# A six-layer cross network on one core: stores of two blocks, eighteen row loads, four more ScalarE parts

## The chip, the cores and the metric

The kernel runs on one core of one Trainium2 chip. Five engines take part: TensorE (PE, and PEld for its weight loads), VectorE (DVE), ScalarE (ACT), GpSimd (POOL) and SyncE (SP), which does no arithmetic and issues transfers. Transfers issued by SP or ACT are carried by the same sixteen DMA engines. The metric is the device time of one execution in microseconds; the median of three runs is compared.

## The reference

The input x0 has 4096 rows of 416 features (26 fields of 16), there are six square weight matrices of 416 x 416 and six bias rows, all in bf16. What is computed is the cross network

```
x = x0
for l in range(6):
    x = x0 * (x @ ws[l] + bs[l]) + x
```

Since every layer multiplies by the same x0, the sum can be kept in a factor c with x = x0 * c: c starts at one, and each layer adds x @ ws[l] + bs[l] to it. The kernel works with this factor.

## The kernel before, in words

**Layout.** In layers 0 to 4 the activations lie transposed: features on the 128 partitions, batch rows along the free axis. The 416 features are three full tiles of 128 (`XM0`, `XH`, `CM`) and a remainder of 32. Four batch groups of 512 rows share the partitions for the remainder (`XR`, `CR`), so its work is done on tiles of 128 partitions. The batch is in two halves `s` of 2048 rows. `CM` and `CR` hold the factor c, `XM0` and `XR[0]` hold x0, and two of the three `XH` buffers hold the present activations.

**Layers 0 to 4.** For each half and each feature tile, TensorE makes the products into PSUM, ScalarE evicts them with the bias as bf16 (L187), and VectorE adds to c (L188) and multiplies by x0 (L189). `rem_pair` does the same for the remainder, through `ew_rem`: there ScalarE evicts a tile of 512 columns in parts of 256 (L196), and VectorE adds (L202) and multiplies (L203) the whole tile. In layers 1 to 3 this comes after the first two feature tiles of the layer. Layer 4 (`feeding_layer`) has its own order, with VectorE's instructions pinned, and also sends c, with the last bias added, through DMA transposes into `XLrows`, where batch rows lie on the partitions.

**The last layer.** Now activations are the stationary operand, so results come out with 128 batch rows on the partitions: a block is 128 rows by 416 features, 104 KB in bf16, and there are 32 of them. They are made in four rounds of eight blocks (u = 0 to 7), each round in four PSUM tiles of two blocks. In rounds one and two (`PAIRS`) two blocks of one tile are evicted together. In round three (`TURNS`) a group is two blocks of two tiles, evicted one by one. In round four (`ENDS`) each block goes through alone, so that the last one has little behind it. The steps of a group are in `ew` and `close_product`: ScalarE copies PSUM to bf16 (L507); VectorE adds c from `XLrows` (L511); when the next group has come to the same point, VectorE multiplies by x0 from `X0rows` into a tile `o` (L494); and the store to the output is issued (L496). For u = 5 to 7 of round four TensorE adds c itself, so that L511 is left out, and for u = 7 VectorE reads PSUM directly (`direct`) and ScalarE issues the store. All other stores are issued by SP.

**Stores.** A store's size is set by `parts`, the blocks per transfer:

```
            for j in range(0, n, parts):
                eng.dma_start(out_v[:, rows(q, g0 + j, parts), :], o[:, j:j + parts, :])
```

`parts` is `n // len(srcs)`. A group evicted at one go is stored in one transfer of two blocks (208 KB): nine of these. The three groups of round three that were evicted in two goes are stored block by block, as are the eight of round four: 14 transfers of 104 KB, 13 by SP and one by ScalarE.

**Order.** Every engine runs its instructions in its own order and waits on semaphores. SP's order is: the transposing loads of x0, weights, `X0rows` in twelve loads (L133), four rows of the last bias (L135), then nothing until layer 4, then eight DMA transposes (L231, L379), then the stores. Transfers take eight completion semaphores in turn; a transfer waits until the one eight before it has landed. The kernel ends (L573) when SP has seen the landing of every transfer and the engines have met.

Of the kernel before, what the change touches and what calls it, by code (L numbers as in the profile page):

```python
# [9 lines left out]
ACT = mybir.ActivationFunctionType  # L10
ALU = mybir.AluOpType
BF16 = mybir.dt.bfloat16
# [4 lines left out]
def kernel(  # L17
# [7 lines left out]
    nc = tc.nc  # L25
    B, D = x0.shape
    L = ws.shape[0]
    P = 128
# [5 lines left out]
    CW = 512  # L34
    SW = NG * CW
    NBT = B // P
# [5 lines left out]
    opool = ctx.enter_context(tc.tile_pool(name="opool", bufs=10))  # L42
# [3 lines left out]
    out_v = out.rearrange("(bt p) d -> p bt d", p=P)  # L46
# [10 lines left out]
    bR = const.tile([P, L], FP32)  # L57
    X0rows = big.tile([P, NBT, D], BF16)
# [14 lines left out]
    def load_wm(eng, l):  # L73
        eng.dma_start(WM[:, l], ws[l, 0:NK * P, :].rearrange("(k p) n -> p k n", p=P))
# [5 lines left out]
    def pin(ins):  # L80
        tc.keep_in_program_order(ins)
# [33 lines left out]
    for g in range(1, NG):  # L115
        dst, src = WR[32 * g:32 * g + 32, 0, :], WR[0:R, 0, :]
# [11 lines left out]
        load_wr(nc.sync, g, 1, L)  # L128
    for l in range(2, L):
        load_wm(nc.sync, l)  # L130
    for q in range(12):
        b0, b1 = NBT * q // 12, NBT * (q + 1) // 12
        nc.sync.dma_start(X0rows[:, b0:b1, :], x0_v[:, b0:b1, :])  # L133
    for g in range(NG):
        nc.sync.dma_start(bLr[32 * g:32 * g + 1, :], bs[LL:LL + 1, :])  # L135
# [55 lines left out]
    def ew_rem(l, s, pr, nxtR):  # L191
        cols = slice(CW * s, CW * s + CW)
        halves = [slice(a, a + CW // 2) for a in range(0, CW, CW // 2)]
        base = CR[:, cols] if l == 0 else tpool.tile([P, 2 * CW], BF16, name="t")
        for a in halves:
            nc.scalar.activation(base[:, a], pr[:, a], ACT.Identity, bias=bR[:, l:l + 1], scale=1.0)  # L196
        if l == 0:
            for a in halves:
                part = slice(CW * s + a.start, CW * s + a.stop)
                pin(nc.vector.tensor_tensor(out=nxtR[:, part], in0=CR[:, part], in1=XR[0][:, part], op=ALU.mult))  # L200
            return
        nc.vector.tensor_tensor(out=CR[:, cols], in0=base[:, 0:CW], in1=CR[:, cols], op=ALU.add)  # L202
        nc.vector.tensor_tensor(out=nxtR[:, cols], in0=CR[:, cols], in1=XR[0][:, cols], op=ALU.mult)  # L203
# [30 lines left out]
    def first_layer(s):  # L234
# [53 lines left out]
        for m in range(2):  # L288
            ew_main(0, s, m, 1, pb[m], nxt)
        ew_rem(0, 0, pr[:, 0, :], nxtR)  # L290
        ew_main(0, s, 2, 1, pb[2], nxt)
        ew_rem(0, 1, pr[:, 1, :], nxtR)

    bias_setup()
# [4 lines left out]
    def rem_pair(l, cur, curR, nxtR):  # L299
        pr2 = psum.tile([P, 2, CW], FP32, tag="ps", name="pr2")  # L300
        for s in range(NS):
            mm_rem(l, s, pr2[:, s, :], cur, curR)
        for s in range(NS):
            ew_rem(l, s, pr2[:, s, :], nxtR)
# [140 lines left out]
    l = LL  # L445
# [8 lines left out]
    def mm_q_open(q, g, py):  # L454
        for k in range(NK):
            for j in range(0, P, 32):
                nc.tensor.matmul(py[j:j + 32, 0:D], lhsT=q_x(q, g, k)[:, j:j + 32], rhs=WM[:, l, k, :],  # L457
                                 start=(k == 0), stop=False, tile_position=(0, j))

    def mm_q_full(q, g, py, closes, adds=False):  # L460
        s, i = quads[q]
        for k in range(NK):
            nc.tensor.matmul(py[:, 0:D], lhsT=q_x(q, g, k), rhs=WM[:, l, k, :],  # L463
                             start=((not closes) and k == 0), stop=(closes and not adds and k == NK - 1))
            if adds:
                c0 = col0(s, g) + 128 * i
                nc.tensor.matmul(py[:, P * k:P * k + P], lhsT=CM[:, k, c0:c0 + 128], rhs=ident[:], start=False, stop=False)
        if adds:
            nc.tensor.matmul(py[:, NK * P:D], lhsT=CR[:, CW * s + 128 * i:CW * s + 128 * i + 128],
                             rhs=ident[:, 32 * g:32 * g + 32], start=False, stop=True)  # L470

    def mm_q_rem(q, py, done):
        s, i = quads[q]
        biased = s == NS - 1 and i >= 2
        for g in range(NG):
            nc.tensor.matmul(py[g][:, 0:D], lhsT=curR[32 * g:32 * g + 32, CW * s + 128 * i:CW * s + 128 * i + 128],  # L476
                             rhs=WR[32 * g:32 * g + 32, l, :], start=(g >= done), stop=(not biased and g < done),
                             tile_position=(32 * g, 0))
        for g in range(NG if biased else 0):
            nc.tensor.matmul(py[g][:, 0:D], lhsT=ones[32 * g:32 * g + 1, :],  # L480
                             rhs=bLr[32 * g:32 * g + 1, :], start=False, stop=(g < done), tile_position=(32 * g, 0))

    pending = []

    def rows(q, g0, n):
        s, i = quads[q]
        b0 = 16 * s + 4 * g0 + i
        return slice(b0, b0 + 4 * (n - 1) + 1, 4)

    def close_product():  # L490
        while pending:
            src, q, g0, n, parts, eng = pending.pop()
            o = opool.tile([P, 2, D], BF16, name="o")
            pin(nc.vector.tensor_tensor(out=o[:, 0:n, :], in0=src, in1=X0rows[:, rows(q, g0, n), :], op=ALU.mult))  # L494
            for j in range(0, n, parts):
                eng.dma_start(out_v[:, rows(q, g0 + j, parts), :], o[:, j:j + parts, :])  # L496

    def ew(q, g0, srcs, eng, added, direct):
        if direct:
            close_product()  # L500
            pending.append((srcs[0], q, g0, 1, 1, eng))
            return
        t = tpool.tile([P, 2 * CW], BF16, name="t")
        n = 0
        for src in srcs:
            w = src.shape[1]
            nc.scalar.copy(t[:, n * D:n * D + w * D].rearrange("p (a d) -> p a d", a=w), src)  # L507
            n += w
        tv = t[:, 0:n * D].rearrange("p (a d) -> p a d", a=n)
        if not added:  # L510
            pin(nc.vector.tensor_tensor(out=tv, in0=tv, in1=XLrows[:, rows(q, g0, n), :], op=ALU.add))  # L511
        close_product()
        pending.append((tv, q, g0, n, n // len(srcs), eng))

    PAIRS = [(0, 0), (0, 1), (1, 0), (1, 1), (2, 0), (2, 1), (3, 0), (3, 1)]
    TURNS = [(0, 0), (0, 1), (1, 0), (2, 0), (3, 0), (1, 1), (2, 1), (3, 1)]
# [2 lines left out]
    for q, at, done in rounds:  # L519
        tiles = [psum.tile([P, 2, CW], FP32, tag="ps", name=f"py{n}") for n in range(4)]  # L520
        bank = [tiles[n][:, a, :] for n, a in at]

        final = q + 2 == NQ

        def close(groups):
            u, direct = groups[0][0], final and groups[0][0] == 7
            srcs = [tiles[at[g[0]][0]][:, at[g[0]][1]:at[g[0]][1] + len(g), 0:D] for g in groups]
            ew(q + u // 4, u % 4, srcs, nc.scalar if direct else nc.sync,
               final and u >= 5, direct)

        for u in range(done):
            if q == 0:
                mm_q_open(q, u, bank[u])
            else:
                mm_q_full(q, u, bank[u], False)
        mm_q_rem(q, bank[0:4], done)
        close([range(done)])
        if q == 0:
            last_rows_out()
        mm_q_rem(q + 1, bank[4:8], 0)  # L540
        for u in range(done, 8):
            mm_q_full(q + u // 4, u % 4, bank[u], True, final and u >= 5)
            if at is ENDS:
                close([[u]])
            elif u % 2:
                close([[u - 1, u]] if at is PAIRS else [[u - 1], [u]])
    close_product()


# [28 lines left out]
```

## Time and profile before

| | |
|---|---|
| median of three runs | 129.44 us (129.32 to 129.5) |
| the profiled execution, its own time | 129.42 us |
| its span, first to last instruction | 127.5 us |
| busy in the span: PE, DVE, ACT | 122.6, 102.4, 87.7 us |
| stores issued by SP, first and last issue | 22, at 111.59 and 124.74 us |
| store issued by ScalarE (u = 7) | at 124.35 us |
| the `X0rows` loads, first issue and length on SP's queue | 23.07 us, 9.20 us |
| largest wait on SP's queue: for layer 4 | 58.1 us |

All positions are microseconds from the start of the span. The execution's own time is 1.9 us above the span. A share of busy time is an average over stages; what matters here is which wait ends last in a stage.

### The profile page before, as it was taken

Reading aid. Unit: us, or ns where it says so; the run is one execution under the profiler, and the core shown is the slowest. Engines: PE = TensorE matmul, PEld = TensorE weight load, DVE = VectorE, ACT = ScalarE, POOL = GpSimd, SP = SyncE. Lnnn points to the kernel's source line nnn. Section 1 sums busy time; section 2 is a strip of 40 time slices with the busy share of each in tenths; the row PEclk is TensorE's granted clock in tenths of the full one; section 3 lists DMA queues with packets and bytes.
Section 4 is the critical chain, followed back from the end, with each engine's and each line's share of the span. In section 5 each row is a group of like instructions: output and inputs, shape, how many; then the busy total and the mean of one; then the engine's idle time right before and its main releaser. Section 6 shows DMA issues by size and latency. Waiting matters only on the chain.

```text
span 127.5 us, 3953 instructions
## 1 busy us (share of the span) xinstructions
PE 122.6 (96%) x1684; PEld 55.3 (43%) x1686; DVE 102.4 (80%) x192; ACT 87.7 (69%) x109; POOL 5.1 (4%) x18
## 2 busy tenths in 40 slices
PE   7999999999999999999999999999999999999970
PEld 3343343444544354434443544354434445445440
DVE  0124579774979898989898989898999999999990
ACT  0138866887858577859577859576859697679650
POOL 4004001400000000000000000000000000000000
PEclk9999999999999999999999999999999999999999
DMA  3999999999950000000000000000097999899864
GB/s 84 256 228 218 184 241 258 295 332 333 338 169 0 5 0 0 8 0 5 0 5 0 5 0 0 5 0 5 0 86 168 173 152 215 177 274 300 264 197 153
DMA packets 42229, 16.37 MB, mean 128 GB/s; under 512 B 31034, under 2 KB 42212, under 8 KB 42212
## 3 DMA queue, kind: packets, MB, share of 16 engines
q1 hardware_dynamic: 37432, 15.40, 53.5%
q10 hardware_dynamic: 4780, 0.72, 3.6%
q8 instruction: 13, 0.21, 0.7%
q14 instruction: 4, 0.03, 0.1%
HBM read 6.15 MB, written 3.41 MB: 75 GB/s over the span
## 4 chain that ended last, share of the span: by engine, by line
PE 90%; DMA 4%; ACTq 2%; DVEq 1%; issue 0%; ACT 0%; DVE 0%
PE pt L208 50%; PE py L463 12%; PE ph L240 11%; PE pt L214 5%; PE pr L224 5%; DMA xrig<-in_x_dram 4%; PE pr L220 2%; PE py L476 2%; PE ph L247 2%; PE py L457 1%; ACTq L86 1%; DVEq L573 1%; ACTq L108 1%; ACT t L507 0%; PE tpr L163 0%
## 5 line engine op out<-in xcount | busy, mean ns | idle before, releaser
L208 PE MATMUL pt<-XH,WM 128*32 128x512 bf16 x1152 | 65.2, 379 | 0.0
L187 ACT ACTIVATE t<-pt,bM 128x1024 bf16<-128x1024 f32 x36 | 37.2, 1116 | 13.7 <-PE pt L214 13.7
L208 PEld LDWEIGHTS <-WM 128*32 128x32 bf16 x1152 | 29.7, 97 | 33.8 <-issue 5.1
L188 DVE TENSOR_TENSOR CM<-t,CM 128x1024 bf16<-128x1024 bf16 x36 | 24.7, 686 | 4.3 <-ACT t L187 4.3
L189 DVE TENSOR_TENSOR XH<-CM,XM 128x1024 bf16<-128x1024 bf16 x36 | 24.9, 692 | 2.6
L507 ACT CAST t<-py 128x416 bf16<-128x416 f32 (+1 forms) x22 | 14.2, 649 | 4.2 <-PE py L463 2.0
L463 PE MATMUL py<-WM,XH 128*128 128x416 bf16 x90 | 17.0, 339 | 0.0
L240 PE MATMUL ph<-XM,WM 128*128 128x512 bf16 x70 | 16.3, 379 | 0.1
L332 ACT ACTIVATE t<-pt,bM 128x1024 bf16<-128x1024 f32 x12 | 12.4, 1115 | 4.1 <-PE pt L214 4.1
L181 ACT ACTIVATE CM<-ph,bM 128x1024 bf16<-128x1024 f32 x12 | 12.5, 1114 | 3.5 <-PE ph L247 3.5
L183 DVE TENSOR_TENSOR XH<-CM,XM 128x512 bf16<-128x512 bf16 x24 | 8.8, 428 | 4.2 <-ACT CM L181 4.2
L463 PEld LDWEIGHTS <-XH 128*128 128x128 bf16 x90 | 8.5, 98 | 7.5 <-issue 1.2
L240 PEld LDWEIGHTS <-WM 128*128 128x128 bf16 x72 | 6.8, 98 | 8.5 <-issue 1.1
L494 DVE TENSOR_TENSOR o<-t,X0rows 128x832 bf16<-128x832 bf16 (+1 forms) x19 | 9.4, 504 | 0.1
L511 DVE TENSOR_TENSOR t<-t,XLrows 128x832 bf16<-128x832 bf16 (+1 forms) x17 | 8.9, 521 | 0.0
L340 DVE TENSOR_TENSOR CM<-t,CM 128x1024 bf16<-128x1024 bf16 x12 | 8.0, 685 | 0.3 <-ACT t L332 0.3
L344 DVE TENSOR_TENSOR XH<-CM,XM 128x2048 bf16<-128x2048 bf16 (+1 forms) x7 | 7.5, 1067 | 0.2
L214 PE MATMUL pt<-XR,WR 32*128 32x512 bf16 x96 | 7.3, 379 | 0.0
L224 PE MATMUL pr<-XH,WM 128*32 128x512 bf16 x96 | 6.6, 379 | 0.0
L196 ACT ACTIVATE t<-pr,bR 128x256 bf16<-128x256 f32 x12 | 4.7, 475 | 1.6 <-PE pr L224 1.6
L114 ACT ACT_TABLE_LOAD x1 | 1.3, 1283 | 6.0 <-DMA XM<-in_x_dram 6.0
L224 PEld LDWEIGHTS <-WM 128*32 128x32 bf16 x120 | 3.2, 97 | 3.2
(61 smaller groups left out, 58.7 us busy)
## 6 DMA issues: line engine op xcount, KB each, us to landing
X0rows<-in_x_dram SPq DMA_DIRECT2D x8, 312.0 KB, 7.3
out_dram<-o SPq DMA_DIRECT2D x9, 208.0 KB, 3.0
WM<-in_ws_dram SPq DMA_DIRECT2D x5, 312.0 KB
out_dram<-o SPq DMA_DIRECT2D x13, 104.0 KB, 2.2
X0rows<-in_x_dram SPq DMA_DIRECT2D x4, 208.0 KB, 6.0
WR<-in_ws_dram SPq DMA_DIRECT2D x4, 130.0 KB, 5.1
WM<-in_ws_dram ACTq DMA_DIRECT2D x1, 312.0 KB
XM<-in_x_dram SPq DMA_TRANSPOSE x8, 5.6
```

What stands on the lines that cost most here:

```text
L181: nc.scalar.activation(c, src, ACT.Identity, bias=bias, scale=1.0)
L187: nc.scalar.activation(t[:], src, ACT.Identity, bias=bias, scale=1.0)
L188: nc.vector.tensor_tensor(out=c, in0=t[:], in1=c, op=ALU.add)
L189: nc.vector.tensor_tensor(out=x, in0=c, in1=XM0[:, m, c0:c0 + 2 * CW], op=ALU.mult)
L208: nc.tensor.matmul(pts[g // 2][32 * q:32 * q + 32, g % 2, :], lhsT=WM[:, l, k, 128 * m + 32 * q:128 * m + 32 * q + 32], rhs=cur[s][:, k, C ...
L214: nc.tensor.matmul(pts[g // 2][:, g % 2, :], lhsT=WR[32 * g:32 * g + 32, l, 128 * m:128 * m + 128], rhs=curR[32 * g:32 * g + 32, CW * s:CW ...
L224: nc.tensor.matmul(pr[32 * g:32 * g + 32, :], lhsT=WM[:, l, k, NK * P:D], rhs=cur[s][:, k, CW * g:CW * g + CW], start=False, stop=(k == NK ...
L240: nc.tensor.matmul(pt[:, gl, :], lhsT=WM[:, 0, k, 128 * m:128 * m + 128], rhs=cur[:, k, c0:c0 + CW], start=(k == 0 and not after_row), sto ...
L332: nc.scalar.activation(ts[t + (h,)][:], pts[t][h][:].rearrange("p a b -> p (a b)"), ACT.Identity, bias=bM[:, t[1], l:l + 1], scale=1.0)
L463: nc.tensor.matmul(py[:, 0:D], lhsT=q_x(q, g, k), rhs=WM[:, l, k, :], start=((not closes) and k == 0), stop=(closes and not adds and k == ...
L494: pin(nc.vector.tensor_tensor(out=o[:, 0:n, :], in0=src, in1=X0rows[:, rows(q, g0, n), :], op=ALU.mult))
L507: nc.scalar.copy(t[:, n * D:n * D + w * D].rearrange("p (a d) -> p a d", a=w), src)
```

## The change

Three edits, which meet only in SP's queue.

The output tile `o` is now taken when a group is closed, not when its product is made, and a store covers the whole tile. So a group of two blocks in round three goes in one transfer. In round four, blocks 0 and 1, 2 and 3, 4 and 5 share a tile each: each product goes into its own half, and the store is issued after the second one. Blocks 6 and 7 are stored alone as before, 7 by ScalarE. SP's stores become 16: fifteen of two blocks and one of one.

`X0rows` is loaded in eighteen transfers (four of one block, fourteen of two) where there were twelve (four of two blocks, eight of three).

In `ew_rem`, the second half's tile (s = 1) in layers 1 and 2 is evicted in four parts of 128 columns where there were two of 256: four more ScalarE instructions in all.

```diff
-    for q in range(12):
-        b0, b1 = NBT * q // 12, NBT * (q + 1) // 12
+    for q in range(18):
+        b0, b1 = NBT * q // 18, NBT * (q + 1) // 18
         nc.sync.dma_start(X0rows[:, b0:b1, :], x0_v[:, b0:b1, :])
...
-        for a in halves:
-            nc.scalar.activation(base[:, a], pr[:, a], ACT.Identity, bias=bR[:, l:l + 1], scale=1.0)
+        n = CW // (4 if s and l in (1, 2) else 2)
+        for a in range(0, CW, n):
+            nc.scalar.activation(base[:, a:a + n], pr[:, a:a + n], ACT.Identity, bias=bR[:, l:l + 1], scale=1.0)
...
-    pending = []
+    pending, outs = [], []
...
     def close_product():
         while pending:
-            src, q, g0, n, parts, eng = pending.pop()
-            o = opool.tile([P, 2, D], BF16, name="o")
-            pin(nc.vector.tensor_tensor(out=o[:, 0:n, :], in0=src, in1=X0rows[:, rows(q, g0, n), :], op=ALU.mult))
-            for j in range(0, n, parts):
-                eng.dma_start(out_v[:, rows(q, g0 + j, parts), :], o[:, j:j + parts, :])
-
-    def ew(q, g0, srcs, eng, added, direct):
+            src, q, g0, n, o, j, last, eng = pending.pop()
+            pin(nc.vector.tensor_tensor(out=o[:, j:j + n, :], in0=src, in1=X0rows[:, rows(q, g0, n), :], op=ALU.mult))
+            if last:
+                eng.dma_start(out_v[:, rows(q, g0 - j, j + n), :], o[:, 0:j + n, :])
+
+    def ew(q, g0, srcs, o, j, last, eng, added, direct):
         if direct:
             close_product()
-            pending.append((srcs[0], q, g0, 1, 1, eng))
+            pending.append((srcs[0], q, g0, 1, o, j, last, eng))
             return
...
-        pending.append((tv, q, g0, n, n // len(srcs), eng))
+        pending.append((tv, q, g0, n, o, j, last, eng))
...
         def close(groups):
-            u, direct = groups[0][0], final and groups[0][0] == 7
+            u = groups[0][0]
             srcs = [tiles[at[g[0]][0]][:, at[g[0]][1]:at[g[0]][1] + len(g), 0:D] for g in groups]
-            ew(q + u // 4, u % 4, srcs, nc.scalar if direct else nc.sync,
-               final and u >= 5, direct)
+            paired = final and u < 6
+            j = u % 2 if paired else 0
+            if not j:
+                outs.append(opool.tile([P, 2, D], BF16, name="o"))
+            ew(q + u // 4, u % 4, srcs, outs[-1], j, bool(j) or not paired, nc.scalar if final and u == 7 else nc.sync,
+               final and u >= 5, final and u == 7)
```

## The prediction

> **What bounds the kernel now.** I read the page's busy times and slices first, then the chain that ended last, then SP's queue and the DMA engines over the last 4 us.
>
> ```profile
> PE 122.6 (96%) x1684; PEld 55.3 (43%) x1686; DVE 102.4 (80%) x192; ACT 87.7 (69%) x109; POOL 5.1 (4%) x18
> ...
> PE   7999999999999999999999999999999999999970
> ...
> 122.91 0.52 ACT t L507
> 123.42 0.02 issue
> 123.44 0.06 DVE o L494
> ```
>
> TensorE is busy without a gap up to 123.6 us; no edit touches its instructions. So only two things can move the time: a new gap in TensorE's row, or the 4 us tail behind it. In the tail the chain leaves TensorE at block u=6's eviction (122.91), goes to its product (123.44), and on to u=7's product and store. SP's queue and the landings stand behind that:
>
> ```profile
> 123.76 0.40 SPq L496 DMA_DIRECT2D out_dram<-o  x1
> ...
> 124.35 0.38 ACTq L496 DMA_DIRECT2D out_dram<-o  x1
> ...
> 124.74 0.39 SPq L496 DMA_DIRECT2D out_dram<-o  x1
> ...
> SPq L573 <- DMA out_dram<-o: 1.3, 3, 0.6
> ```
>
> The store at 124.74 is u=6's, yet its product ended at 123.44 + 0.38 = 123.82. SP was late: it issued u=0 to u=6 at 121.86, 122.30, 122.77, 123.26, 123.76, 124.25, 124.74, one per 0.44 to 0.49 us, each after the one before and not after its product. By the semaphore events, u=7's store (124.35) has landed at 126.31, u=6's at 126.63; SP's last waits follow at 126.64 and 126.70, and the span ends at 127.50, 0.87 us after the last landing. The end is therefore the issue backlog of SP.
>
> One thing limits what an earlier issue can bring. The sixteen DMA engines are not level:
>
> ```profile
> DMA  0006994269963799628993199952999999999600
> GB/s 17 25 25 216 415 308 125 75 216 308 291 167 92 233 291 283 200 92 275 333 325 92 50 283 275 275 158 92 308 374 316 333 366 341 283 275 300 208 25 0
> ```
>
> These are the DMA engines from 122.4 to 126.4 us in slices of 0.1 us: bursts of some 0.35 us, one per store, with valleys between, until the last three run together from 125.1. In the valley at 122.4 one engine alone still moves (17 to 25 GB/s). It fell behind at 116.34, when an instruction fetch of 16 KB took one engine for 0.95 us: of the sixteen parts of the ninth store (issued 117.79) fifteen have landed by 120.04, the last at 121.39. From there that part comes at 121.70, 122.03, 122.36, 122.67, 123.04, 123.44, 124.13 (u=0; another fetch of 0.31 us began at 122.81), 124.50 (u=1), 124.81, 125.15, 125.53 (u=4). Only at u=4 has it caught up with the other fifteen (125.51).
>
> **The change part by part.**
>
> Round three: 10, 11 and 12 lose one SP issue each (0.33 to 0.45 us). They are issued as soon as their product is ready, and that stays (118.51, 119.57, 120.44); the second halves leave up to 0.42 us earlier. Nothing waits for them.
>
> Round four, SP's queue: seven issues become four. A two-block issue costs 0.42 to 0.46 us in the rows at 112.65 to 114.26, a one-block issue 0.33 to 0.41. The products end at u=1 121.66, u=3 122.80, u=5 123.37, u=6 123.82, and a store starts 0.03 us after its product when SP is free. So: u0+1 at 121.69, u2+3 at 122.83, u4+5 at 123.40, free at 123.85, u6 at 123.90 instead of 124.74, a move of 0.84 us. Only u=2's data leaves later, by 0.06 us. There is a 0.44 us hole in SP's queue ahead of u=0's store (121.42 to 121.86, product long done) that the trace doesn't name. If it falls on u4+5 instead, u6 goes at 124.34, still ahead of u=7's store. A slower issue under full DMA queues (0.97 and 1.23 us at 111.59 and 116.47) bounds it from above: +0.8 us on u4+5 puts u6 back at 124.7, no gain; I take 0.45, since the last seven issues all cost 0.33 to 0.41.
>
> The end by the last landing: u=7's store depends on its product (124.31) and stays at 124.35. On fifteen engines it landed by 126.28 with u=5's burst beside it, so 126.1 to 126.3 now; 1.74 us, the shortest flight in the tail, would be 126.09. On the lagging engine everything after u=1 (124.50) is now queued early: six blocks at 0.315 us each (steps of 0.31 to 0.33 while it was never idle; a pair saves one completion write of 0.009) end at 124.50 + 1.89 = 126.39. Bounds: 0.33 a block gives 126.48, no lag 126.28. I take 126.39, as that engine shows these very steps. u=7's semaphore is waited for last, so the wait at 126.64 falls away: 126.39 + 0.81 = 127.20, against 127.50: −0.30 us.
>
> The Trainium skill's "DMA: Bandwidth & Descriptors", section "Anatomy of one DMA — SWDGE (gpsimd) path", gives a transfer a fixed 2.0 us plus bytes over 436 GB/s, mostly the receipt of the last write: an estimate of 2.24 us for one block. By it u=7 would land at 126.59 and the change bring 0.04 to 0.10 us. Here one-block stores issued by SP from 122.77 on took 1.74 to 2.04 us, so the rule, given for another issuing path, is too long for them.
>
> Row loads: six more issues on SP. Twelve took 9.20 us from 23.07, one each 0.47 to 1.22 us; in that stretch the engines are full (some 330 GB/s), so the bytes, unchanged, set the pace. Six more cost between 0 and 6 x 0.9 = 5.4 us of SP's queue; I take 1. Behind them on SP stand the bias rows (needed at 118.5) and the first transpose at 92.84, before which SP waits 58.1 us; the rows are first used at 108.8. That cover makes the cost nothing; without it, up to 5.4 us. POOL issues no transfer.
>
> The completion semaphores are taken in turn, and six more loads and six fewer stores leave u=7 on the one it had. ScalarE's wait on it was met at 123.44, 0.9 us ahead of need; now it is that of store nine, 121.39. With 17 instead of 20 output tiles over ten buffers, reuse waits get shorter too.
>
> ScalarE parts: no 128-column eviction is in the trace. Of the neighbours, 256 columns start every 0.36 us, 1024 every 1.0, which extrapolates to 0.25. Four of 0.25 for two of 0.36 is +0.28 us per layer; bounds 0 and +0.72 (each as long as 256). It ends ahead of these idle times:
>
> ```profile
> 36.95 2.12 ACT L187 ACTIVATE t<-pt,bM 128x1024 bf16<-128x1024 f32 x2 [1.33 <-PE pt L214]
> ...
> 36.64 0.42 DVE L202 TENSOR_TENSOR CR<-t,CR 128x512 bf16<-128x512 bf16 x1
> ...
> 56.18 1.11 ACT L187 ACTIVATE t<-pt,bM 128x1024 bf16<-128x1024 f32 x1 [1.33 <-PE pt L214]
> ```
>
> ScalarE then waits 1.33 us for TensorE, and the add that consumes the parts starts at 36.64, 1.0 us after the last part ended (35.62). Cost nothing; if the cover failed, TensorE would wait for a PSUM buffer by what exceeds it.
>
> Sum: 129.42 − 0.30 = **129.12 us**, 0.32 below the median of 129.44 (which is 0.02 above the profiled execution), or 0.25%. About 0.2%, 0.26 us, is what can be told from no change.
>
> **The rivals.**
>
> A (the forecast): the backlog goes, the lagging engine sets the end. With the bounds above, 126.28 + 0.81 to 126.48 + 0.87: 129.01 to 129.27 us.
>
> B: the lagging engine isn't behind any more when u=7 comes. For it: it had caught up at u=4 before. Against: it had idle time only by the backlog that now goes. Then u=7's own flight is all: 126.09 + 0.81, −0.6 at most: 128.82 to 129.01.
>
> C: nothing is won, because u=7's store flies longer among the pairs. For it: u=0 and u=1 took 2.27 and 2.20 us. At 2.2 us it lands at 126.55, −0.14 by the same working; u4+5's issue stretched by 0.8 us brings u6 back to where it was, 0. A few hundredths either way: 129.2 to 129.6. The 2.24 us of the Trainium skill's "DMA: Bandwidth & Descriptors", above, would be this case.
>
> D, the other side: the pair u4+5 is still in flight when u6 and u7 come. For it: two-block stores took 2.6, 2.8 and 3.2 us, the ninth 3.6. On its slowest engine u6 and u7 follow it 0.32 us apart. With u4+5 (issued 123.40) in flight for 2.6 us they end at 126.64, level with before; from 2.9 us (126.94, +0.25 us) the kernel is slower, and 3.3 us gives 127.34, +0.65. Against: those stores flew among transposes and a fetch, at 300 GB/s. 129.7 to 130.1.
>
> E, that the change isn't made as said, is excluded by the code: `last` is true for every group but the first of a pair.
>
> **How the numbers follow.** A 0.50, of which 0.42 lies below 129.18 and 0.08 above; B 0.13; C 0.18; D 0.19. Faster by over 0.2%: 0.42 + 0.13 = 0.55. Within: 0.08 + 0.18 = 0.26. Slower: 0.19. The time is A's. The range runs from 128.88, inside B, to 129.60, the top of C, and leaves out D and B's low end. The faster cases alone span 128.82 to 129.18.
>
> **What would show it.** Right: 16 stores on SP, u6's issued near 123.9; the last landing u=7's, at 126.3 to 126.5, its sixteenth part trailing; no gap in TensorE's row; the loads of `X0rows` over long before 92. Wrong: an SP issue beyond 0.6 us after 122.8; a last landing after 126.6; TensorE waiting for PSUM near 37 or 56 us; TensorE's end away from 123.6, which would mean that the order of instructions has changed elsewhere.

## The result

| | before | after |
|---|---|---|
| median of seven runs | 129.50 us (129.32 to 129.66) | 129.01 us (128.89 to 129.24) |
| ratio, with its 95% interval | | 0.9964 [0.9952, 0.9976] |
| profiled execution, its own time | 129.42 us | 129.12 us |
| its span; time outside the span | 127.52; 1.90 us | 127.34; 1.78 us |
| start of u=7's product on VectorE | 123.73 us | 123.98 us |
| from there to the span's end, here called the tail | 3.79 us | 3.36 us |

The change makes the kernel faster, by 0.36%. The median lies 0.11 us under the predicted 129.12 us and inside the range. That the profiled execution also took 129.12 us is chance: the table shows that it started its end 0.24 us later than the profile of before, and gained 0.43 us in the tail and 0.12 us outside the span. The forecast of 0.30 us was for the tail alone.

The busy times of the page of after, its stores and its row loads, and then ScalarE's new parts from the groups by form (busy time, mean ns, idle time before them):

```profile
PE 122.9 (97%) x1684; PEld 55.3 (43%) x1686; DVE 102.4 (80%) x192; ACT 88.3 (69%) x113; POOL 5.1 (4%) x18
...
out_dram<-o SPq DMA_DIRECT2D x15, 208.0 KB, 2.9
...
L197 ACT ACTIVATE t<-pr,bR 128x128 bf16<-128x128 f32 x8 | 2.3, 381 | 0.0
```

TensorE has the same 1684 products; the order of instructions on every engine is that of before apart from the edits. ScalarE has four more instructions and 0.6 us more work, beside TensorE.

SP's stores at the end of after, one row each from the timeline (start us, length us), and ScalarE's store of u=7:

```profile
120.71 0.37 SPq L496 DMA_DIRECT2D out_dram<-o  x1
121.93 0.37 SPq L496 DMA_DIRECT2D out_dram<-o  x1
123.07 0.37 SPq L496 DMA_DIRECT2D out_dram<-o  x1
123.64 0.37 SPq L496 DMA_DIRECT2D out_dram<-o  x1
124.11 0.43 SPq L496 DMA_DIRECT2D out_dram<-o  x1
124.59 0.38 ACTq L496 DMA_DIRECT2D out_dram<-o  x1
```

These are group 12 of round three, u=0 and 1, 2 and 3, 4 and 5, 6, and 7. SP now starts each after its product, and u=6's store leaves ahead of u=7's. The landings confirm that u=7's comes last, at 126.51 us; u=6's came at 126.18.

The DMA engines of after from 122.6 to 126.6 us, in slices of 0.1 us (share in tenths, then GB/s):

```profile
DMA  0049999951000189999999999899999989700000
GB/s 17 25 166 366 358 349 349 358 175 25 0 0 0 58 291 308 308 283 308 341 308 308 308 300 341 300 308 317 333 358 325 283 275 291 215 8 0 0 0 0
```

What matters are the three empty slices from 123.6 to 123.9 us. There all sixteen engines have run dry, the late one too. From then on they are full until 126.0 us and end together: no slices with one engine alone (17 to 25 GB/s) follow, but for one of 8 GB/s.

The last waits of SP on landings, from 123 us on: in all, number of times, longest.

```profile
SPq L577 <- DMA out_dram<-o: 1.8, 4, 0.6
```

SP ends them at 126.59 us, 0.08 us after the last landing; in before it was 126.77, 0.14 us after.

Below, positions from different profiles are compared by shifting each so that u=7's product starts at 123.73 us, as in before; such a position is called relative.

### The profile page after: what moved, and what is told of

Its sections match the earlier page's. It is cut to its first block, busy times and chain, and to the rows that moved or that the text cites. A ratio compares the mean times of both kernels' runs of the same rounds, so it can differ in the third digit from the quotient of the medians.

```text
span 127.3 us, 3951 instructions
## 1 busy us (share of the span) xinstructions
PE 122.9 (97%) x1684; PEld 55.3 (43%) x1686; DVE 102.4 (80%) x192; ACT 88.3 (69%) x113; POOL 5.1 (4%) x18
## 4 chain that ended last, share of the span: by engine, by line
PE 90%; DMA 5%; SPq 1%; DVEq 1%; ACT 0%; issue 0%; DVE 0%
PE pt L209 50%; PE py L464 12%; PE ph L241 11%; DMA XM<-in_x_dram 5%; PE pt L215 5%; PE pr L225 5%; PE pr L221 2%; PE py L477 2%; PE ph L248 1%; SPq L78 1%; PE py L458 1%; DVEq L577 1%; ACT t L507 0%; PE py L481 0%; PE py L468 0%
## 5 line engine op out<-in xcount | busy, mean ns | idle before, releaser
L209 PEld LDWEIGHTS <-WM 128*32 128x32 bf16 x1152 | 29.7, 97 | 33.8 <-issue 5.1
L197 ACT ACTIVATE t<-pr,bR 128x256 bf16<-128x256 f32 (+1 forms) x16 | 5.3, 427 | 1.6 <-PE pr L225 1.6
```

The source lines that it names most:

```text
L209: nc.tensor.matmul(pts[g // 2][32 * q:32 * q + 32, g % 2, :], lhsT=WM[:, l, k, 128 * m + 32 * q:128 * m + 32 * q + 32], rhs=cur[s][:, k, C ...
```

## The experiments

All medians; each ratio is against runs of the kernel before on the same chip (129.41 to 129.53 us). Tail and time outside the span are of the profiled executions.

| kernel | median us | ratio [95%] | tail us | outside us |
|---|---|---|---|---|
| before | | 1 | 3.79 | 1.90 |
| after | 129.01 | 0.9964 [0.9952, 0.9976] | 3.36 | 1.78 |
| loads_only | 129.59 | 1.0012 [1.0004, 1.0021] | 3.94 | 1.87 |
| stores_only | 129.77 | 1.0027 [1.0018, 1.0037] | 4.02 | 1.86 |
| parts_only | 130.05 | 1.0047 [1.0031, 1.0063] | 4.30 | 1.78 |
| no_parts | 129.00 | 0.9973 [0.9963, 0.9983] | 3.35 | 1.87 |
| u6_by_act | 129.46 | 1.0006 [0.9998, 1.0015] | 3.86 | 1.81 |
| loads10 | 129.50 | 1.0007 [0.9998, 1.0016] | 4.05 | 1.78 |
| loads26 | 128.95 | 0.9961 [0.9948, 0.9974] | 3.36 | 1.78 |
| round3_15 | 129.06 | 0.9968 [0.9955, 0.9981] | 3.48 | 1.79 |
| pair45_16 | 128.78 | 0.9944 [0.9931, 0.9957] | 3.25 | 1.81 |
| pair45_noparts | 128.95 | 0.9958 [0.9943, 0.9973] | 3.29 | 1.88 |
| filler48 | 131.16 | 1.0126 [1.0106, 1.0146] | 4.08 | 1.78 |
| lanes_plus2 | 131.43 | 1.0147 [1.0121, 1.0173] | 3.68 | 1.78 |

The last two start their end 1.5 and 2.5 us late through their own edits; only their tails are read.

**What was to be told apart.** In before SP stands for 0.44 us ahead of u=0's store, and an instruction fetch of 8 KB follows on one DMA engine, 0.95 us after the stand's end. In after the stand is ahead of group 12's store (120.18 to 120.63), whose product ends at 120.65 only, with the fetch at 121.33. So the first theory was that the stand has a fixed place in SP's stream of instructions, and that the number of loads and stores ahead decides what it hits. The rival gives its place no part in the time. Later theories were numbered as they came up; each is told with its runs. Over all runs the place is borne out: in each of the fourteen profiles of the table there is a gap of 0.44 to 0.45 us ahead of the 80th instruction that is recorded for SP (issues and semaphore waits counted), wherever that falls in the program.

### The loads alone, the stores alone

loads_only is before with this edit; stores_only is after without it and without the parts.

```
-    for q in range(12):
-        b0, b1 = NBT * q // 12, NBT * (q + 1) // 12
+    for q in range(18):
+        b0, b1 = NBT * q // 18, NBT * (q + 1) // 18
```

> The kernel before with only the eighteen loads of x0's rows; every store as before. Theory 1 (the wait of 0.4 us in SP's queue that no semaphore explains sits at a fixed place in SP's instruction stream, here at its 80th recorded instruction, and six more loads move it six instructions forward in the program's stores, away from block u=0): it appears ahead of the store of group 11 of round three, where 0.25 us of it delays anything; u=6's store is issued 0.3 us earlier against the end of TensorE's work than before, close to u=7's, and the time is 0.2 to 0.35 us below before, with no change to any store. Theory 2 (loads are hidden and the gain is all in the pairs): no change within 0.1 us, the wait ahead of u=0 still there.

> The changed kernel with the twelve loads and the two ScalarE parts of before; only the stores in pairs. Theory 1 (the wait has a fixed place in SP's stream): six instructions later in the program than in the changed kernel, so it falls between the stores of u=2+3 and u=4+5; u=4+5 leaves some 0.25 us after its product, u=6 likewise, and the time is 0.3 to 0.45 us below before, 0 to 0.15 us above the changed kernel. Theory 2: the pairs carry the whole gain, equal to the changed kernel within 0.05 us, and the wait stays ahead of u=0+1.

The stand moved as the first theory says, both ways. With more instructions ahead it fell in round three (119.53 to 119.99 in loads_only, fetch at 120.62); with fewer it fell ahead of u=4 and 5 (123.35 to 123.80 in stores_only, fetch at 124.65). SP's stores in stores_only:

```profile
122.98 0.37 SPq L496 DMA_DIRECT2D out_dram<-o  x1
...
123.88 0.38 SPq L496 DMA_DIRECT2D out_dram<-o  x1
...
124.36 0.41 SPq L496 DMA_DIRECT2D out_dram<-o  x1
```

The third, u=6's, still leaves at relative 124.20, half a microsecond ahead of before, and yet the kernel is slower than before. The DMA engines from 122.6 to 127 us, in slices of 0.11 us, and the fetch among the packets:

```profile
DMA  0599998200029999983189999999999830000000
GB/s 23 189 348 355 363 363 273 61 0 0 0 76 310 295 325 310 318 265 113 45 265 310 310 303 325 295 348 348 326 280 287 265 121 23 23 0 0 0 0 0
...
q14 instruction: 1, 0.01, 0.4%
```

The fetch took one engine for 0.31 us when the others were full. Fifteen parts of u=7's store had landed at relative 126.46, the sixteenth at 126.75; the two slices of 23 GB/s at the end are that engine alone. By the first theory the two kernels were to be 0.2 to 0.45 us faster than before; neither expectation had this fetch. Then the final wait grew, in both kernels:

```profile
SPq L577 <- DMA out_dram<-o: 2.1, 1, 2.1
```

This row is stores_only's from 123 us on: one wait of 2.1 us met last, with the others still to be passed. SP was through 0.25 us after the last landing in stores_only and 0.27 us in loads_only, against 0.08 in after. loads_only won nothing by freeing u=0, because there the backlog of SP begins earlier: from 120.4 us on it issues about every 0.5 us, and u=6's store leaves at relative 124.76, as in before.

```profile
119.99 0.33 SPq L496 DMA_DIRECT2D out_dram<-o  x1
...
120.90 0.49 SPq L496 DMA_DIRECT2D out_dram<-o  x1
...
123.91 0.40 SPq L496 DMA_DIRECT2D out_dram<-o  x1
...
124.89 0.39 SPq L496 DMA_DIRECT2D out_dram<-o  x1
```

So the first theory had the place right and the price wrong. The cost is not the stand alone, but what follows it (one DMA engine lost for a while) and the order of the last semaphores.

### Without the parts, and u=6 moved to ScalarE

no_parts is after with the old halves, `n = CW // 2`; u6_by_act is before with

```
-            ew(q + u // 4, u % 4, srcs, nc.scalar if direct else nc.sync,
+            ew(q + u // 4, u % 4, srcs, nc.scalar if final and u >= 6 else nc.sync,
```

> The changed kernel without the four more ScalarE parts. Theory 1 and 2 alike: they end ahead of an idle 1.3 us of ScalarE and cost and bring nothing: equal to the changed kernel within 0.1 us. Rival: they shift ScalarE's own stream by four instructions and with it a wait near the end; then the last store by ScalarE leaves up to 0.4 us after its product here.

> The kernel before with one edit: u=6's store is issued by ScalarE, as u=7's is; no pairs, twelve loads. Theory 1 (SP's backlog of issues sets the end, not the size or number of the transfers): u=6's store leaves 0.05 us after its product and lands before u=7's, and the time is 0.3 to 0.45 us below before, equal to the changed kernel. Rival (larger transfers are what helps, since the DMA engines work better on them): no gain, or under 0.1 us.

Without the parts the tail is the same, 3.35 us; the difference of the medians can't be told from nothing, though the time outside the span is 0.09 us longer.

u6_by_act brings u=6's store to relative 123.85, the place that the prediction wanted for it, and wins nothing. u=6 landed at 125.90. But u=5's, still in SP's backlog, was issued at 124.22 and landed at 126.26, and u=7's, behind both, at 126.57, after a flight of 2.22 us. The last landing came 0.06 us earlier than in before, and SP was through 0.12 us earlier. But ScalarE, with two more instructions at its end, came 0.28 us late to the final meeting of the engines, and that ate the gain; the cause is a stand of its own, told below with ScalarE's stream. So this run's median doesn't price the early issue alone. Its landing does: 0.06 us, against 0.36 in after. One early issue isn't enough, the bytes ahead of u=7 have to be early too, and the pairs do that.

### How many loads: 10, 18, 26

Both are after, with another count of row loads.

```
-    for q in range(18):
-        b0, b1 = NBT * q // 18, NBT * (q + 1) // 18
+    for q in range(10):
+        b0, b1 = NBT * q // 10, NBT * (q + 1) // 10
```

> The changed kernel with ten loads of x0's rows where it has eighteen. Eight fewer leave every completion semaphore where it is, and move the fixed place in SP's instruction stream eight instructions later, from the store of group 12 to that of u=6. Theory 3 (at that place SP stands for 0.4 us and some 0.8 us later one DMA engine is taken for 0.3 us by the fetch of SP's next 8 KB of instructions; both cost only where the last stores are under way): u=6's issue moves by 0.3 to 0.4 us but stays ahead of u=7's data, so that fifteen parts of u=7 land as in the changed kernel; the fetch begins near 125.3, and the sixteenth part lands 0.25 to 0.35 us later. Time 0.25 to 0.4 us above the changed kernel, 129.25 to 129.45. Rival (only the transfers' sizes and the order of the final waits matter): equal to the changed kernel within 0.05 us.

> The changed kernel with twenty-six loads of x0's rows. Completion semaphores as with eighteen; the fixed place in SP's stream moves eight instructions forward, to the stores of round two or the start of round three, its fetch to before 120. Theory 3: nothing in the tail is touched; equal to the changed kernel within 0.1 us, the last store's sixteen parts landing together. Rival (more and smaller loads slow or hasten something in themselves): the difference between ten and eighteen loads continues, 0.1 us or more.

With 26 the stand falls ahead of the last store of round two (116.53 to 116.98, fetch at 118.42) and the time is that of after. With 10 it falls ahead of u=6:

```profile
123.25 0.37 SPq L496 DMA_DIRECT2D out_dram<-o  x1
...
124.15 0.35 SPq L496 DMA_DIRECT2D out_dram<-o  x1
```

and 0.5 us is lost, the whole gain. The DMA engines from 123 to 127 us, in slices of 0.1 us:

```profile
DMA  6100017999999999999769999996000000000000
GB/s 192 33 0 0 0 58 266 316 308 266 300 383 283 308 316 308 316 291 300 208 192 406 366 275 266 300 250 199 8 25 17 25 0 0 0 0 0 0 0 0
...
q14 instruction: 2, 0.02, 1.0%
```

Fifteen parts of u=7's store landed at relative 126.33, the sixteenth 0.62 us later; the slices of 8 to 25 GB/s are that one engine. Two fetches hit it, at 125.18 and at 125.80 us. The second was not expected, and it led to ScalarE, below. That ten, eighteen and twenty-six loads carry the same bytes and differ by where the stand falls shows that the loads matter through SP's stream alone.

### Which stores have to be paired

round3_15 pairs round three only, with 15 loads; pair45_16 pairs round three and u=4 and 5, with 16 loads. The loads keep the stand out of the end.

```
-            paired = final and u < 6
+            paired = False                     # round3_15
+            paired = final and u in (4, 5)     # pair45_16
```

> The changed kernel with pairs in round three only: the eight blocks of round four are stored one by one, as before; fifteen loads, so that the last store keeps its completion semaphore. Theory 4 (SP's backlog forms where round three's single stores and the 0.4 us wait run into round four's): with round three in pairs SP is free when round four begins, u=0 to u=3 leave with their products, u=6 leaves at 124.3 by the clock of the kernel before instead of 124.74, level with u=7, and the time is 0.25 to 0.4 us below before. Rival (seven single issues in round four are too many by themselves): u=6 leaves 0.2 us or more after u=7's store, time within 0.15 us of before.

> The changed kernel with only u=4 and 5 of round four in one store, u=0 to 3 alone; sixteen loads, so that the last store keeps its completion semaphore. In the changed kernel the DMA engines stand empty from 123.6 to 123.9, because u=2 waits for u=3, and are full from there to the end. Theory 4: u=2's data leave 0.57 us earlier, the engines are less full at the end, and u=7's store lands 0.05 to 0.15 us earlier: 128.85 to 129.0. Rival (u=7's own flight from 124.35 is what is left): equal to the changed kernel within 0.05 us.

round3_15 is as good as after within the intervals, although SP's last seven stores run without a pause again (relative 121.31 to 124.27). They start 0.55 us earlier than in before, because three issues fewer in round three leave SP free at 120.84 us: the stand (120.84 to 121.28) then passes while u=0's product, which ends at 121.25, is still being made, where in before it came after it. pair45_16 is the best kernel of the study, 0.56% faster than before; its interval and that of after overlap. Its last stores, and the DMA engines from 123.2 to 126.7 us in slices of 0.09 us:

```profile
122.81 0.37 SPq L496 DMA_DIRECT2D out_dram<-o  x1
123.38 0.38 SPq L496 DMA_DIRECT2D out_dram<-o  x1
123.85 0.42 SPq L496 DMA_DIRECT2D out_dram<-o  x1
...
DMA  5998639995004999999999999988700000000000
GB/s 181 285 285 257 181 95 314 333 342 153 10 0 143 295 323 304 323 314 314 295 305 314 380 343 305 285 257 257 208 0 0 0 0 0 0 0 0 0 0 0
```

u=0 to 3 go one by one as their products come, so the engines are all but empty for two slices only, near 124.1 us, less is left for the last 2 us (u=4 to 7, where after has u=2 to 7), and u=7 landed at relative 126.14 instead of 126.26, after a flight of 1.80 us instead of 1.92.

### ScalarE's stream: the parts alone, and the best kernel without them

parts_only is before with the edit of `ew_rem` alone; pair45_noparts is pair45_16 with `n = CW // 2`.

```
-        for a in halves:
-            nc.scalar.activation(base[:, a], pr[:, a], ACT.Identity, bias=bR[:, l:l + 1], scale=1.0)
+        n = CW // (4 if s and l in (1, 2) else 2)
+        for a in range(0, CW, n):
+            nc.scalar.activation(base[:, a:a + n], pr[:, a:a + n], ACT.Identity, bias=bR[:, l:l + 1], scale=1.0)
```

> The kernel before with only the four more ScalarE parts. So far profiles without them have 1.86 to 1.90 us of the execution outside the span, and a fetch of ScalarE's instructions at 128 us or later, after the span; profiles with them have 1.78 to 1.81 us, and that fetch at 125.7 to 126.1, under the last stores. Theory 5 (ScalarE's stream has such a place too, and the parts move it from behind the end to where ScalarE only waits): 1.78 to 1.81 us outside the span, the fetch near 126; time 0.1 us below before, less what the fetch adds to u=6's sixteenth part (0 to 0.3 us): 129.35 to 129.65 with before at 129.45. Rival (the parts do nothing): 1.86 to 1.90 us outside, no change.

> The best kernel so far (pairs in round three and for u=4 and 5, sixteen loads) without the four ScalarE parts. Theory 5: 1.86 to 1.90 us outside the span, the fetch of ScalarE's instructions after 128, 0.05 to 0.1 us above the 128.78 of the kernel with them. Rival: equal, 1.78 to 1.81 us outside.

ScalarE's own stream has such a place too, ahead of the 192nd instruction that is recorded for it. In six of the seven kernels with the four parts (filler48, below, is the other) that is a stand of 0.32 to 0.33 us behind u=7's store (in after 124.97 to 125.29 us), and then a fetch of 8 KB follows: at 126.07 us in after, 126.01 in parts_only, 125.69 in pair45_16. In u6_by_act, with two instructions more, the stand is 0.36 us long and lies in the final meeting (126.97 to 127.33 us), with the fetch at 127.96. In the five kernels with neither, before among them, ScalarE has 191 recorded instructions in the span, one short of the place, and that fetch comes after the span (128.0 to 128.9 us). Where the last store is all but through when it comes, it costs nothing. In parts_only it isn't; the DMA engines from 126 us, in slices of 0.05 us:

```profile
DMA  9889864100100000000000000000000000000000
GB/s 414 266 250 316 250 200 134 50 17 17 33 17 0 17 0 0 0 0 0 0 0 0 0 0 0 0 0 0 0 0 0 0 0 0 0 0 0 0 0 0
...
q14 instruction: 1, 0.01, 1.1%
```

Data of u=6's store, late by SP's backlog, still move until 126.3 us, and one engine goes on alone. Fifteen parts landed at 126.77, the sixteenth at 127.21: +0.44 us, more than was expected. The same window of after, for the difference (126 to 127.3 us, slices of 0.03 us):

```profile
DMA  6390000000000000000000000000000000000000
```

All was through at 126.1 us. The parts also come with a shorter time outside the span: 1.78 to 1.81 us in the nine profiles in which ScalarE has at least two instructions more than in before, 1.86 to 1.90 in the five others, which are those with the place still ahead at the span's end. That their stand then falls outside the span would fit, but no row shows it. Against that, pair45_noparts is 0.17 us slower than pair45_16 and no_parts level with after; the intervals overlap, so the medians don't settle whether that 0.1 us is won.

### The late engine, and the last semaphores

filler48 is after with other warm-up products at the start, so that TensorE's stream has 45 more; lanes_plus2 is after with one load of weights in three pieces (two more transfers), and the parts in one layer only.

```
-    pe_filler(3, CW)
+    pe_filler(48, 32)                          # filler48
...
-        nc.scalar.dma_start(WR[0:R, 0, :], ws[0, NK * P:D, :])
+        for a, b in ((0, 128), (128, 256), (256, D)):      # lanes_plus2
+            nc.scalar.dma_start(WR[0:R, 0, a:b], ws[0, NK * P:D, a:b])
...
-        n = CW // (4 if s and l in (1, 2) else 2)
+        n = CW // (4 if s and l == 1 else 2)
```

> The changed kernel with 48 warm-up products of 32 columns where there are three of 512, all of them unused by the result: 90 more records in TensorE's stream ahead of all other work. The fetch of 16 KB for TensorE at 116.5 moves to 109 to 112. The step of the prediction (that fetch puts one DMA engine behind, and its part of each store trails): with it gone from there, the sixteenth part of the stores of round three lands within 0.5 us of the fifteenth, where it trails by 0.5 to 1.4 us in the changed kernel; the last store is as before, since the lag is over by then: the stretch from u=7's product to the end of the span stays at 3.36 us within 0.05. Rival (the lag has another source): the sixteenth parts trail as before. The opening may move by some tenths, which is no part of the question.

> The changed kernel with the small load of the remainder's weights for layer 0 on ScalarE's queue in three pieces instead of one, and two ScalarE parts fewer, so that the length of SP's and ScalarE's streams is unchanged but every later transfer takes its completion semaphore two places on. u=7's semaphore then stands in the second of SP's five final waits instead of the fifth. Theory 6 (each final wait costs 0.06 us also when it is met, and what follows the last landing is paid in full): SP's drain comes 0.25 us after the last landing instead of 0.08, the stretch from u=7's product to the end of the span is 3.50 to 3.60 us instead of 3.36, with landings as in the changed kernel. Rival: the order of these waits is free, 3.36 us.

In filler48 TensorE's 16 KB fetch left the stores' time (116.5 us) for 108.95, and the sixteenth parts of the last three two-block stores of round three trail by 0.09, 0.05 and 0.27 us instead of 1.36, 0.93 and 0.46. So that fetch is what puts one engine behind, as the prediction read it. The tail, though, grew to 4.08 us where 3.36 was expected. The DMA engines from 125 to 129 us, in slices of 0.1 us:

```profile
DMA  0059999999999998579999861000000000000000
GB/s 0 0 166 390 283 258 258 349 325 283 308 333 300 316 333 250 133 258 358 375 316 275 283 225 34 25 25 17 0 0 0 0 0 0 0 0 0 0 0 0
```

A fetch started at 125.39, relative 123.90, when the stores of u=2 to 6 had been issued and u=7's was still to come, and all of them end with one part 0.54 to 0.76 us late. It fits ScalarE's: the edit left ScalarE one semaphore wait more, so that its 192nd recorded instruction is u=7's store itself, and a stand ahead of that can't be told from the wait for u=7's product. So a fetch of 8 KB under full engines is costly, and its place was not controlled here. In lanes_plus2 SP was through 0.25 us after the last landing, as expected from the turn of the semaphores; its tail, 3.68 us, was 0.08 us over the range because the landing itself was late by 0.14. There too ScalarE has two semaphore waits more, against what was expected, and a fetch came at relative 123.26; whether the late landing is its doing was not tried.

## Why the prediction was right, and where it was wrong

**SP's backlog: right.** The issues were foreseen at 121.69, 122.83, 123.40 and 123.90 us; relative they came at 121.69, 122.83, 123.40 and 123.86. u=7's stayed at 124.35. A two-block issue cost 0.37 us, not 0.45.

**The lagging engine: the step that failed.** "On the lagging engine everything after u=1 (124.50) is now queued early: six blocks at 0.315 us each", ending at 126.39. Its part of u=0 and 1 landed at relative 123.87, not 124.50. Group 12's part was 0.18 us earlier than in before, and SP's fetch, which in before came at 122.81 and fits the step of 0.69 us to u=0's part, had come at 121.33; no step of this part in after, 0.53 to 0.71 us for two blocks, shows it, so which engine it took isn't known. Then it ran dry with the rest (the three empty slices above): the store of u=2 and 3 was issued at relative 122.83, but its data moved only 0.9 us later, a delay that the step left out. The trailing of the sixteenth parts shrank to 0.14, 0.04 and 0.01 us. So no engine lags, and the end is u=7's flight on all sixteen. That is rival B's condition, but not its price: B took the shortest flight, 1.74 us, and here it was 1.92, behind engines that are full with u=2 to 6 from 123.9 us on; pair45_16, with less queued ahead, had 1.80. The relative landing of 126.26 is close to the bound of 126.28 that the step gave for "no lag". The landing is 0.36 us earlier than before's, where 0.24 was forecast, and the tail 0.43 us shorter, where 0.30 was. Two readings of the step were off besides: the late part's steps in before reach 0.40 us while it still trails by 0.74 (122.67, 123.04, 123.44), not 0.33; and the span of before ends at 127.52 us, so 0.87 is 0.90 and 0.81 is 0.84, which cancels in the difference.

By the Trainium skill's "DMA: Bandwidth & Descriptors", section "Anatomy of one DMA — SWDGE (gpsimd) path", given there for transfers that GpSimd issues, the flight would be 2.24 us, an estimate. u=7's, issued by ScalarE, took 1.92 us in after, 1.80 in pair45_16, and 2.22 in u6_by_act behind two other stores; so the traces lie under it where little is queued ahead.

**The final wait: right, and worth more than was said.** The step kept u=7 on the semaphore that SP waits for last, and so took 0.06 us off. loads_only and stores_only, whose count of transfers breaks that order, lost 0.13 and 0.11 us against before. Six loads added and six stores removed cancel in the turn of eight.

**Loads at nothing: wrong in effect.** Their own time is hidden, as worked out: the eighteen took SP 11.90 us instead of 9.20, where 1 us more was taken, and SP still waits 58.5 us for layer 4. But they are instructions of SP, and their number decides what SP's stand and the fetch behind it hit. The prediction saw the 0.44 us hole, and held it harmless even on u=4 and 5, with u=6 then at 124.34. stores_only had just that, with u=6 at 124.20, and was 0.27% slower than before: the fetch behind the hole and the final waits are what was missing.

The Trainium skill's "Runtime: NRT & Kernel Launch", section "Instruction fetch mechanics", has the sequencer fetch blocks of 16 KiB ahead of need, so that crossing a block is mostly hidden. TensorE's fetches of 16 KB agree in that it doesn't stand for them; the fetches that follow the stands of SP and ScalarE here are of 8 KB, and the stands take 0.32 to 0.45 us. In after, the three fetches among the stores take a DMA engine for 0.51 to 0.96 us.

**Parts at nothing: right for the eviction, wrong for the stream.** The parts of 128 columns start every 0.25 us, as extrapolated, take 381 ns each and lie in ScalarE's idle time. So this edit doesn't meet the others in SP's queue, as the description of the change has it: it acts through ScalarE's stream. Alone, the parts cost 0.6 us; in the profile the tail is 0.51 us longer, 0.44 of it by ScalarE's fetch in the last stores. Behind the pairs they cost nothing.

So the gain is that of the stores and the loads together. Alone each edit makes the kernel slower: by 0.27% (stores), 0.12% (loads), 0.47% (parts). Stores and loads without the parts (no_parts) have the tail of after and are 0.27% faster than before, all three 0.36%, with overlapping intervals. The stores take SP's backlog away, the loads keep SP's stand and fetch off the last stores and the final waits in order, and the early end makes ScalarE's fetch harmless. The prediction had the first of these, and added the others at zero; it came out near because here they don't hit, which is luck as far as the prediction goes. Rivals C and D did not come: the pair of u=4 and 5 was in flight for 2.21 us, u=7 for less than 2.2.

**What stays open.** That the stand is a fetch boundary is inferred: from its fixed place in the stream and the fetch that follows it in every profile, 0.63 to 1.44 us after SP's, not from a row that says so. Which DMA engine a fetch takes is not recorded. Why the time outside the span is shorter where ScalarE has more instructions was seen, but its cause not shown. pair45_16 beats before clearly (128.73 to 128.82 us); against after it is 0.23 us ahead with overlapping intervals.

## What to carry to other kernels

In the last microseconds, count the instructions on each queue, and not only their durations: an edit that is hidden by its time can still move a stand of 0.4 us and an instruction fetch onto the last stores, so look in the trace for holes in the issuing queues that nothing explains and for fetches, and try one or two instructions more or less. Combine transfers where the issuing queue is behind (about 0.4 us an issue, for one block or for two), but leave apart those that can go earlier while engines are idle. And see which completion semaphore the last transfer takes, since the end of the kernel waits for them in turn.

## What had not been expected of the hardware

**A fetch on one engine holds up a whole store.** 8 KB took 0.31 to 0.63 us among the stores, 0.31 also with full engines (stores_only); in the last stores it put the sixteenth part 0.26 to 0.76 us behind the other fifteen.

**Waits that are already met still cost.** Each of SP's last waits takes about 0.06 us; with four of them behind the last landing SP was through after 0.25 us instead of 0.08.

**The start varies from run to run.** u=7's product started between 123.59 and 124.10 us in profiles whose beginning no edit touched. From TensorE's first product into a tile `pt` (26.25 us in before) to u=7's product it is 97.47 to 97.48 us in all fourteen profiles, so the spread arises before that. The speed of TensorE's very first products varies too: from 4 to 6 us the rows count eleven in the profile of before and six in that of after, though the granted clock is given as 1.00 in all of them (us from and to, the length, PE busy, PEld, DVE, ACT, POOL, the granted clock, DMA share, GB/s). First before, then after:

```profile
4.00:5.00 1.00, 1.00 (x4) 0.35 (x3) 0.00 (x0) 0.00 (x0) 0.24 (x1) 1.00 1.33 259
5.00:6.00 1.00, 0.96 (x7) 0.42 (x6) 0.34 (x2) 0.03 (x1) 0.01 (x1) 1.00 1.36 229
```

```profile
4.00:5.00 1.00, 1.00 (x3) 0.30 (x2) 0.00 (x0) 0.00 (x0) 0.00 (x0) 1.00 1.32 256
5.00:6.00 1.00, 1.00 (x3) 0.15 (x1) 0.00 (x0) 0.00 (x0) 0.26 (x1) 1.00 1.36 205
```

But that doesn't set the start of the end: pair45_16 also has six in these rows, and its u=7 started at 123.72 us, as in before; loads26 has twelve, and started at 124.02. What does stays open. That spread of 0.5 us is as large as the gain, so two single profiles can't be compared by their ends; here the tails were.
